# Mamba2 scan and low-rank mixer on one core: batch 0's up product by split halves

## The chip, the cores and the metric

The kernel runs on one core of a Trainium2 chip. The metric is the device time of one execution in microseconds. Before the change three runs took 219.5, 219.6 and 219.62 us; their median is 219.6 us.

The engines are named as in the profile: PE is TensorE (PEld its weight loads), DVE is VectorE, ACT is ScalarE, POOL is GpSimd, SP is SyncE, which here only issues DMAs.

## The reference

Two stages follow each other. The first is a chunked state-space scan over 4 batches, 8 heads, 768 positions, head size 32, state size 16. The second is a mixer over the tokens and a two-layer network over the channels:

```python
xt = x.transpose(0, 2, 1)
h = xt @ U @ V                      # over 768 positions, rank 32
u = x + h.transpose(0, 2, 1)        # (4, 768, 256)
ch = np.maximum(u @ w_ch1, 0.0) @ w_ch2   # 256 -> 1024 -> 256
return (u + ch).astype(np.float32)
```

The weights U, V, w_ch1 and w_ch2 reach the kernel as 64-bit floats, so each of their numbers is two 32-bit words in memory, and the kernel turns them into 32-bit numbers itself, by masks, integer operations and products on the two words.

## The kernel before

**An order written out by hand.** The kernel is under manual scheduling. A string PLAN of some 630 words is followed word by word (`follow`, L875); each word calls one function that emits a few instructions. Every engine runs its own instructions in that order, and waits only for the results it needs. So moving a word in PLAN moves its instructions on every engine's queue, and moving a load moves it on SP's queue.

**The scan.** The 768 positions of a batch are three pairs of blocks, so there are twelve pairs k = 0 to 11, three per batch. Words for pair k: `b` and `x` load B, C and x (SP); `P` (or `Q`, a part of it) scales B and C by decays into BC (`prep`, L471); `T` transposes BC on PE and ScalarE copies it out (L483); `g` is the gram product, `m` and `M` its causal masks on VectorE (L518, L531); `s` the chunk states and `u` their update, on VectorE, with a masked copy Sm made by GpSimd (L548, L563); `i`, `n`, `j` are products into the output y, with a tiny GpSimd copy `settled` (L590) that holds `j` behind `i`; `y` and `t` copy and transpose the result.

**The mixer.** Per batch b (`mixer`, L684): `p`, `q`, `a` apply U and V and add to u. Then come the up product (1024 columns as eight blocks m of 128, over two halves j of 384 tokens) and the down product `d` (L787). For batches 1 to 3 a 32-bit number is held as three parts, near, far and both, so that a product is made by three one-pass products in place of one plain 32-bit product, which runs in several passes. `S` (L730) splits u into these parts (one ScalarE, two VectorE instructions); `f` (L762) makes the first two products, two matmuls each, and ScalarE multiplies the sum in PSUM by 1 + EPS; `e` (L768) adds the third product and ScalarE takes the Relu; `h` and `J` split the result for the down product. Batch 0 before the change has a plain up product `U` (L751), two 32-bit matmuls for each (j, m), which appear as four instructions, and ScalarE takes the Relu; its down product is plain too (`PLAIN = 2`).

**Weights.** `W` and `w` load pieces of w_ch1 and w_ch2, 512 KB each but for two of 256 KB. `c` converts a piece to 32 bits, one step of the generator `to_fp32` (L412) for each word c: two masks on VectorE and a conversion on ScalarE; then the exponent on ScalarE; then two VectorE operations; then the product. Pieces c0 and c2 are the first quarter of w1 (columns 0 to 255, which are m = 0 and 1), c3 to c5 the other three quarters, c1 is U and V, c6 to c9 are the first four quarters used of w2. `R` (`refine`, L445) makes the parts near, far and both out of a converted quarter; R0 to R3 are w1's, R4 to R7 w2's, all for batches 1 to 3. Temporaries, loaded words and Relu results share fifteen buffers called `words`; the converted w1 (`w1f`) shares one buffer with u's parts.

The VectorE is reached through a wrapper, so that all VectorE instructions have line L162 in the profile. Line L740 is the matmul inside `products`, for U, f, e and d alike.

Of the kernel before, what the change touches and what calls it, by code (L numbers as in the profile page):

```python
# [10 lines left out]
FP32 = mybir.dt.float32  # L11
# [3 lines left out]
WCOLS = 512  # L15
# [19 lines left out]
    'b0.0 b0.1 b0.2 x0.0 x0.1 b1.0 b1.1 b1.2 ')  # L35
PLAN = (
# [43 lines left out]
def kernel(  # L80
# [185 lines left out]
    def load_w(n):  # L266
        if n < 2:
            if "w" not in own:
                own["w"] = words_of(w1f[0])
# [175 lines left out]
    def refine(c):  # L445
# [11 lines left out]
        if c >= NQ:  # L457
            yield
            far = low.bitcast(FP32)
            both.append(w2c(n, FP32R))  # L460
# [464 lines left out]
```

## Time and profile before

The page of the profile shows one execution, which took 220.41 us from outside; its span, from the first to the last instruction, is 218.7 us. In the tables of stretches the columns are the bounds in us, the length, the busy time (and number of instructions) of PE, PEld, DVE, ACT and POOL, the granted clock, the DMA share and GB/s. In rows of a timeline the columns are the start, the length, the engine, the line, what is written and read, the shape and the number of instructions merged; a merged row's length runs to the end of the last. In rows of groups the numbers behind the bar are the busy time in us and the mean of one in ns.

| what | us |
|---|---|
| median of the runs | 219.6 |
| the profiled execution, from outside | 220.41 |
| its span | 218.7 |
| TensorE busy in the span | 210.3 |
| VectorE busy | 154.0 |
| ScalarE busy | 114.2 |
| GpSimd busy | 17.7 |

Matmuls overlap, and their ends are modelled. So a matmul's cost is read from start to start, not from its length. On VectorE and ScalarE consecutive instructions overlap by a little under 0.1 us, so sums of their lengths are a little too long.

### The profile page before, as it was taken

How to read it: one execution, taken by the hardware profiler on the slowest of the kernel's cores; microseconds unless marked ns; L12 is line 12 of the kernel's file. 1: busy time of each engine (PE TensorE's matmuls, PEld its weight loads, DVE VectorE, ACT ScalarE, POOL GpSimd, SP SyncE). 2: the span in 40 equal slices, each digit the busy share in tenths (PEclk: the TensorE clock that was granted, in tenths of full speed). 3: DMA queues.
4: the chain of work that ended last, by engine and by line, in shares of the span. 5: the costliest groups of instructions: out<-in, count | busy, mean ns of one | idle time of the engine just before them, and what ended most of it. 6: DMA issues, size and time to landing. Idle time of an engine off the chain costs nothing.

```text
span 218.7 us, 6992 instructions
## 1 busy us (share of the span) xinstructions
PE 210.3 (96%) x2988; PEld 182.4 (83%) x2988; DVE 154.0 (70%) x330; ACT 114.2 (52%) x261; POOL 17.7 (8%) x41
## 2 busy tenths in 40 slices
PE   7999899999899999999999999999999999999993
PEld 4667566665677889998998999999999999999992
DVE  4687689999983996349796697566575945757813
ACT  3335967798357554645555458153565364466220
POOL 6021020010300210002120000100000000000000
PEclk9999999999999999999999999999999999999999
DMA  6986879896082170080000450100000010100003
GB/s 87 132 118 150 152 103 330 233 207 88 3 124 47 19 132 4 18 126 3 27 3 1 53 118 0 51 10 24 0 0 24 17 34 3 48 3 22 3 24 120
DMA packets 69519, 14.56 MB, mean 67 GB/s; under 512 B 63793, under 2 KB 67697, under 8 KB 69489
## 3 DMA queue, kind: packets, MB, share of 16 engines
q1 hardware_dynamic: 69488, 14.13, 32.5%
q8 instruction: 23, 0.38, 0.8%
q14 instruction: 8, 0.06, 0.1%
HBM read 10.98 MB, written 3.15 MB: 65 GB/s over the span
## 4 chain that ended last, share of the span: by engine, by line
PE 83%; DVE 11%; issue 2%; ACT 1%; DMA 1%; POOL 0%; DVEq 0%; POOLq 0%; ACTq 0%
PE x L740 27%; PE z L740 22%; PE y L740 12%; DVE words L162 5%; PE y L651 3%; PE y L629 3%; PE x L525 2%; PE w L671 2%; DVE M L162 2%; PE w L494 2%; DVE S L162 2%; PE w L557 1%; PE z L525 1%; PE w L694 1%; DMA a_sb<-in_a_dram 1%
## 5 line engine op out<-in xcount | busy, mean ns | idle before, releaser
L162 DVE SCALAR_TENSOR_TENSOR words<-words 128x768 fp32r<-128x768 f32 (+6 forms) x44 | 33.8, 799 | 0.3
L740 PE MATMUL x<-u,w 128*128 128x384 f32 x144 | 32.1, 342 | 0.0
L740 PE MATMUL z<-u,w 128*128 128x384 f32 x144 | 32.1, 342 | 0.0
L740 PEld LDWEIGHTS x<-u,w 128*128 128x128 f32 x144 | 24.6, 188 | 0.4 <-issue 0.2
L740 PEld LDWEIGHTS z<-u,w 128*128 128x128 f32 x144 | 24.3, 188 | 0.4 <-issue 0.2
L740 PE MATMUL x<-w2c,words 128*128 128x256 f32 x112 | 22.8, 339 | 0.7 <-DVE w2c L162 0.7
L745 ACT ACTIVATE x<-x 128x384 f32<-128x384 f32 (+1 forms) x30 | 13.6, 454 | 18.8 <-PE x L740 17.3
L745 ACT ACTIVATE z<-z 128x384 f32<-128x384 f32 (+1 forms) x27 | 12.5, 463 | 18.3 <-PE z L740 14.5
L740 PE MATMUL y<-w,words 128*128 128x256 f32 x144 | 20.3, 280 | 0.0
L740 PEld LDWEIGHTS x<-w2c,words 128*128 128x128 f32 x112 | 18.2, 189 | 2.4 <-DVE w2c L162 0.9
L162 DVE SCALAR_TENSOR_TENSOR words<-x,words 128x384 fp32r<-128x384 f32 x24 | 13.0, 552 | 9.7 <-ACT words L774 9.6
L740 PEld LDWEIGHTS y<-w,words 128*128 128x128 f32 x144 | 19.2, 188 | 0.0
L162 DVE SCALAR_TENSOR_TENSOR words<-z,words 128x384 fp32r<-128x384 f32 x24 | 12.8, 550 | 6.7 <-ACT words L774 6.7
L740 PE MATMUL x<-w,words 128*128 128x256 f32 x96 | 14.3, 285 | 0.0
L585 POOL TENSOR_TENSOR Sm<-S,own 128x256 f32<-128x256 f32 (+1 forms) x12 | 8.1, 676 | 76.3 <-DVE S L162 44.7
L774 ACT ACTIVATE words<-x 128x384 fp32r<-128x384 f32 x24 | 11.4, 488 | 5.6 <-PE x L740 5.6
L774 ACT ACTIVATE words<-z 128x384 fp32r<-128x384 f32 x24 | 11.3, 492 | 5.0 <-PE z L740 5.0
L162 DVE SCALAR_TENSOR_TENSOR S<-S,kept,w 128x64 f32<-128x64 f32 x40 | 11.2, 279 | 2.8 <-PE w L557 0.9
L740 PEld LDWEIGHTS x<-w,words 128*128 128x128 f32 x96 | 12.9, 189 | 0.1
L740 PE MATMUL z<-w2c,words 128*128 128x256 f32 x56 | 11.5, 339 | 0.2 <-DVE S L162 0.2
L651 PE MATMUL y<-M,x 64*32 64x64 f32 x768 | 10.5, 225 | 1.0 <-issue 0.9
L663 ACT COPY yT<-y 128x256 f32<-128x256 f32 x24 | 7.8, 380 | 6.9 <-PE y L629 6.9
(154 smaller groups left out, 400.0 us busy)
## 6 DMA issues: line engine op xcount, KB each, us to landing
words<-in_moe_w_ch_dram SPq DMA_DIRECT2D x7, 512.0 KB, 5.2
x<-in_x_dram SPq DMA_DIRECT2D x24, 128.0 KB, 3.4
out_dram<-ytok SPq DMA_DIRECT2D x24, 128.0 KB, 1.7
bc<-in_B_dram SPq DMA_DIRECT2D x24, 64.0 KB, 3.0
bc<-in_C_dram SPq DMA_DIRECT2D x12, 128.0 KB, 3.2
words<-in_moe_w_ch_dram SPq DMA_DIRECT2D x2, 256.0 KB, 3.7
words<-in_moe_V_dram SPq DMA_DIRECT2D x4, 48.0 KB, 1.9
words<-in_moe_U_dram SPq DMA_DIRECT2D x1, 192.0 KB, 4.0
```

What stands on the lines that cost most here:

```text
L162: self.last = call(*args, **kwargs)
L494: nc.tensor.transpose(out=tp[:, i, v], in_=s["BC"][:, i, c + v].rearrange("p h n -> p (h n)"), identity=ident)
L525: nc.tensor.matmul(out=g[r][cols, c], lhsT=s["T"][rows, 0, c, cols], rhs=s["Cm"][rows, :, :, ts(2 * c + p, Q)].rearrange("r v t i -> r v i ...
L557: nc.tensor.matmul(out=s["A"][p][ts(r, Q), v], lhsT=s["BC"][half, 0, v, 2 * r:2 * r + 2].rearrange("p h n -> p (h n)"), rhs=x_sb[k][half, ...
L585: nc.gpsimd.tensor_tensor(out=s["Sm"][:, sl], in0=s["S"][:, sl].rearrange("p i (s d) -> p i s d", s=2), in1=own2[:, b, 4 * q:4 * q + sl.st ...
L629: product = nc.tensor.matmul(out=y[p][ts(r % 2, H), r // 2, c], lhsT=own[ts(r, Q)], rhs=s["T"][ts(r, Q), 1, :, ts(2 * c + p, Q)].rearrange ...
L651: product = nc.tensor.matmul(out=y[p][ts(i, Q), n, c], lhsT=x_sb[k][half, c, h], rhs=s["M"][half, h // 2, c, h % 2], start=fresh(k, p, [i] ...
L663: nc.scalar.copy(out=yp[:, :, :, p], in_=st[k]["y"][p])
L671: nc.tensor.transpose(out=t[:, c, g], in_=yT[b][:, g, ts(2 * q + c, P)], identity=ident)
L740: nc.tensor.matmul(out=t, lhsT=lhsT, rhs=rhs, start=start, stop=True, skip_group_check=True)
L745: nc.scalar.activation(t, t, AF.Copy, scale=1.0 + EPS)
L774: nc.scalar.activation(gs[j, m // 2][0][:, m % 2], t, AF.Relu, scale=NEAR)
```

## The change

Three things change at once.

1. **Batch 0's up product.** For m = 2 to 7 the plain `U` becomes `f` and `e` as in the other batches, with `S0.0` and `S0.1` in front; the Relu's result isn't split, because batch 0's down product stays plain. For m = 0 and 1 `U` remains. So 4 `U`, 12 `f` and 12 `e` stand where 16 `U` stood. The pieces c3 to c5 are no longer converted to one 32-bit number: a new generator `to_parts` makes near, far and both from the two words directly, in six steps. `R1`, `R2` and `R3` go. The first quarter is converted as before into `w1f`, now one of the fifteen `words` buffers.
2. **Additions on GpSimd.** In `to_parts` an integer addition and the difference for both; in `to_fp32` of the w2 pieces (`aside`) an integer addition in place of VectorE's addition; in `refine` both differences (now four steps); and `prep` of pairs 4 to 11.
3. **Order.** The whole PLAN from the second line on. Among it the loads: W3, W2 and W4 stand ahead of most of b4, b5 and x4, and c4 is begun before c3.

```diff
+SCALED = range(4, 12)
 PLAN = (
...
-    w1all = mix.tile([P, NQ, NCB, W], FP32, tag="u", name="w1f", bufs=1)
-    w1f = [w1all[:, c] for c in range(NQ)]
+    w1f = raw.tile([P, 2 * WCOLS], INT32, tag="words", name="w1f", bufs=NWORDS).bitcast(
+        FP32)[:, :NCB * W].rearrange("p (c m) -> p c m", c=NCB)
...
+        if aside:
+            nc.gpsimd.tensor_tensor(out=rest, in0=top, in1=rest, op=ALU.add)
         nc.scalar.activation(power, e, AF.Relu, bias=bias[:p], scale=8.0)
         yield
-        vector.scalar_tensor_tensor(out=rest, in0=top.bitcast(FP32), scalar=-7.0 * 2 ** 20,
-                                       in1=rest, op0=ALU.add, op1=ALU.add)
+        if not aside:
+            vector.scalar_tensor_tensor(out=rest, in0=top.bitcast(FP32), scalar=-7.0 * 2 ** 20,
+                                           in1=rest, op0=ALU.add, op1=ALU.add)
...
+    def to_parts(dst, words):
...
+        vector.tensor_scalar(out=head, in0=hi, scalar1=0x7ffffe00, scalar2=None,
+                                op0=ALU.bitwise_and)
+        vector.tensor_scalar(out=low, in0=hi, scalar1=0x1ff, scalar2=3,
+                                op0=ALU.bitwise_and, op1=ALU.logical_shift_left)
+        nc.scalar.activation(rest, lo.bitcast(UINT32), AF.Copy, scale=2.0 ** -29)
+        yield
+        nc.gpsimd.tensor_tensor(out=rest, in0=low, in1=rest, op=ALU.add)
+        nc.scalar.activation(power, head, AF.Relu, bias=bias[:p], scale=8.0)
+        yield
+        vector.scalar_tensor_tensor(out=power, in0=hi, scalar=-2 ** 31, in1=power,
+                                       op0=ALU.bitwise_and, op1=ALU.bitwise_or)
+        yield
+        nc.scalar.copy(out=near, in_=wide(power.bitcast(FP32)))
+        vector.tensor_scalar(out=head, in0=power, scalar1=-2 ** 23, scalar2=None,
+                                op0=ALU.bitwise_and)
+        yield
+        vector.scalar_tensor_tensor(out=far, in0=wide(rest), scalar=2.0 ** -11,
+                                       in1=wide(head.bitcast(FP32)), op0=ALU.mult, op1=ALU.mult)
+        yield
+        nc.gpsimd.tensor_tensor(out=both, in0=wide(power.bitcast(FP32)), in1=far.bitcast(FP32),
+                                op=ALU.subtract)
+        yield
...
-        vector.tensor_tensor(out=far, in0=w, in1=near.bitcast(FP32), op=ALU.subtract)
+        nc.gpsimd.tensor_tensor(out=far, in0=w, in1=near.bitcast(FP32), op=ALU.subtract)
+        yield
         nc.scalar.activation(low, far, AF.Copy, scale=1.0 / EPS)
...
+        nc.gpsimd.tensor_tensor(out=both[0], in0=near.bitcast(FP32), in1=low.bitcast(FP32),
+                                op=ALU.subtract)
...
-            vector.tensor_tensor(
+            (nc.gpsimd if k in SCALED else vector).tensor_tensor(
                 out=part, in0=bc_sb[k].rearrange("p h i c n -> p (i c) h n")[:, g],
...
         def second(j, m):
 
+            t = gs["t", j, m]
+            products(t, terms(j, m, (2,)), False)
+            if not (b or j >= PLAIN):
+                if (j, m // 2) not in gT:
+                    gT[j, m // 2] = pair(FP32)
+                nc.scalar.activation(gT[j, m // 2][:, m % 2], t, AF.Relu)
+                return
```

The stretch of PLAN on which the prediction dwells, from the first up product on, reads before (to its last up product):

```
U0.0.0 m4 c4 U0.0.1 P5 c4 c5 U0.1.0 U0.1.1 c5 w7 B6 U0.1.3 T5 M4 U0.1.2 s4 u4.0 c4 n4 u4.1 s5 c6 R1 R0
c5 L7 u5.0 T5 c9 u5.1 c7 U0.0.2 c5 c9 c7 U0.1.5 c7 c6 c6 c6 U0.0.3 U0.0.4 U0.1.4 U0.1.6 c8 P6 c8 U0.0.6
c8 U0.1.7 c7 d0.1.2.0 c8 c9 i4 g5 m5 T6 c9 d0.1.2.1 d0.1.2.2 T6 L8 M5 d0.1.2.3 U0.0.5 n5 R0 i5 P7 j4 g6
y4.0 X6 y4.1 R1 R3 j5 t4 d0.1.1.0 M6 P8 y5.1 T7 m6 y5.0 R2 R5 U0.0.7
```

and after:

```
U0.0.0 c4 c4 c3 T4 T4 c4 U0.1.0 P5 c3 U0.0.1 U0.1.1 f0.0.4 w5 X5 c5 c5 c3 g4 t3 e0.0.4 B6 m4 c3 f0.0.5
c5 M4 c3 f0.0.2 c5 s4 n4 T5 T5 e0.0.2 c5 u4.0 u4.1 c5 f0.0.6 e0.0.5 f0.0.7 i4 c6 R0 g5 j4 y4.0 M5 c6
y4.1 P6 e0.0.6 m5 c6 f0.0.3 s5 u5.0 w6 n5 c6 T6 u5.1 e0.0.7 T6 d0.0.0.0 e0.0.3 i5 R4 g6 w7 m6 w8 S0.1 j5
c7 y5.0 y5.1 t4 M6 d0.0.1.0 c7 L7 f0.1.2 P7 f0.1.3 t5 L8 f0.1.7 c7 f0.1.6 f0.1.4 d0.1.0.0 c8 e0.1.3 c8 c9
c7 e0.1.2 e0.1.6 d0.0.0.1 f0.1.5 d0.0.1.1 c8 c8 e0.1.7 e0.1.5 p1 c9 X6 T7 c9 d0.0.2.0 c9 e0.1.4
```

More of the change, by code (lines that the diff above doesn't have):

```diff
@@ L268, in load_w @@
             if "w" not in own:
-                own["w"] = words_of(w1f[0])
-            dst, t = w1f[0][:, :, ts(n, P)], own["w"][:, ts(n, 2 * NCB * P)]
+                own["w"] = words_of(w1[0][:, :, ts(0, W)])
+            dst, t = w1f[:, :, ts(n, P)], own["w"][:, ts(n, 2 * NCB * P)]
             weights[2 * n] = dst, t
@@ L274, in load_w @@
         elif n <= NQ:
-            load_words(n + 1, w1f[n - 1], w13[:, :, ts(n - 1, 2 * quarter)])
+            dst = each(w1, every, every, ts(n - 1, W))
+            t = words_of(dst[0])
+            weights[n + 1] = dst, t
+            begin(out=t.rearrange("p (i j) -> p i j", i=NCB),
+                  in_=w13[:, :, ts(n - 1, 2 * quarter)])
         else:
@@ L449, in refine @@
             w2, every, ts(n, 2))
-        w = (w1f if c < NQ else w2f)[n]
+        w = w1f if c < NQ else w2f[n]
+        if c >= NQ:
+            both.append(w2c(n, FP32R))
         nc.scalar.activation(near, w, AF.Copy, scale=NEAR)
@@ L749, in pair, with terms @@
             return t.bitcast(dtype)[:, :2 * HS].rearrange("p (m t) -> p m t", m=2)
+        def terms(j, m, which):
+            return [(w1[v][:, n, ts(m, P)], us[j][v][:, n]) for v in which for n in range(NCB)]
         def plain(j, m):
@@ L755, in plain @@
             t = bank("xz"[m % 2], HS)
-            products(t, [(w1f[m // 2][:, n, ts(m % 2, P)], block(n, j)) for n in range(NCB)], True)
+            products(t, [(w1f[:, n, ts(m, P)], block(n, j)) for n in range(NCB)], True)
             nc.scalar.activation(gT[j, m // 2][:, m % 2], t, AF.Relu)
-        def terms(j, m, which):
-            return [(w1[v][:, n, ts(m, P)], us[j][v][:, n]) for v in which for n in range(NCB)]
         def first(j, m):
```

44 lines of the change are left out of this document (28 added, 16 removed), and 75 rows, old and new, of the table PLAN.

## The prediction

> **What bounds the kernel now.** I read the profile page's engine shares and its chain of waits first, then the busy time by stretches, then the waits of TensorE.
>
> ```profile
> span 218.7 us, 6992 instructions
> PE 210.3 (96%) x2988; PEld 182.4 (83%) x2988; DVE 154.0 (70%) x330; ACT 114.2 (52%) x261; POOL 17.7 (8%) x41
> PE 83%; DVE 11%; issue 2%; ACT 1%; DMA 1%; POOL 0%; DVEq 0%; POOLq 0%; ACTq 0%
> ...
> 30.00:40.00 10.00, 9.79 (x111) 6.30 (x93) 9.09 (x22) 7.28 (x17) 0.52 (x1) 1.00 0.99 257
> 34.90:67.70 32.80, 32.09 (x414) 21.26 (x413) 30.35 (x66) 23.06 (x48) 3.85 (x4) 1.00 0.70 149
> ...
> PE x L740 <- DVE w2c L162: 0.7, 1, 0.7
> ```
>
> TensorE holds 83% of the chain. Batch 0's sixteen plain up products (U) lie between 34.9 and 67.7 us, and in that stretch TensorE misses only 0.7 of 32.8 us, at full clock; its one long wait there is for a down weight of VectorE (0.7 us). So TensorE's own work sets the end, and work taken off it counts in full as long as nobody starves it. But VectorE is 93% busy there (30.35 of 32.8), and DMA 99% from 30 to 40 us: the feeding engines are close behind.
>
> **TensorE's gain.** The two ways of multiplying stand side by side in the trace, as start-to-start times.
>
> ```profile
> 48.48 5.32 PE L740 MATMUL x<-yT,w1f 128*128 128x384 f32 x16
> 53.64 1.45 PE L740 MATMUL z<-yT,w1f 128*128 128x384 f32 x4
> ...
> 88.09 0.86 PE L740 MATMUL z<-u,w 128*128 128x384 f32 x4
> 88.79 0.51 PE L740 MATMUL x<-u,w 128*128 128x384 f32 x2
> 89.13 0.86 PE L740 MATMUL z<-u,w 128*128 128x384 f32 x4
> ```
>
> A plain product is 4 instructions; 16 of them take 53.64 - 48.48 = 5.16 us, so one product 1.29 us. The split one, as batch 1 makes it, is 4 instructions (0.70) and then 2 (0.34): 1.04 us. Twelve of sixteen change: 12 x (1.29 - 1.04) = 3.0 us; by the finer 0.174 us of one instruction, 12 x 0.245 = 2.94 us, which I take. The four left plain stay at 1.29.
>
> **What that asks of ScalarE.** New: 12 rescalings in PSUM between f and e, two S (near part of u), three copies of w1's near part. Gone: the two passes of R1, R2 and R3.
>
> ```profile
> L745 ACT ACTIVATE x<-x 128x384 f32<-128x384 f32 x24 | 11.4, 476 | 17.5 <-PE x L740 16.3 <-ACT yT L663 0.8 <-DVE words L162 0.2
> L757 ACT ACTIVATE words<-x 128x384 f32<-128x384 f32 x8 | 3.7, 489 | 0.0
> L735 ACT ACTIVATE u<-yT 128x768 fp32r<-128x768 f32 x6 | 5.0, 839 | 3.3 <-DVE yT L162 3.3
> L451 ACT ACTIVATE w<-w1f 128x512 fp32r<-128x512 f32 x4 | 2.4, 637 | 0.0
> ```
>
> 12 x 0.476 + 2 x 0.839 + 3 x 0.637 - 3 x 2 x 0.637 (the second pass of R has the same size as the first) = +5.5 us over the kernel. If all of it fell on the old stretch, ScalarE would hold 23.06 + 5.5 = 28.6 us against TensorE's 32.8 - 2.94 = 29.9; the end still belongs to TensorE, with only 1.3 us to spare. Each new half product has f, a rescaling, e and a Relu in a row, 0.476 + 0.489 = 0.97 us of ScalarE beside 1.04 of TensorE, so ScalarE now paces almost as tightly as TensorE; that is a rival below.
>
> **VectorE's relief.** The removed and added instructions:
>
> ```profile
> L162 DVE TENSOR_TENSOR BC<-bc,F 128x512 f32<-128x512 f32 x9 | 6.2, 684 | 0.5 <-issue 0.5
> L162 DVE TENSOR_TENSOR words<-w1f,w 128x512 f32<-128x512 f32 x4 | 2.7, 682 | 0.0
> L162 DVE SCALAR_TENSOR_TENSOR w<-words,w 128x512 fp32r<-128x512 f32 x4 | 3.1, 766 | 0.1
> L162 DVE SCALAR_TENSOR_TENSOR w2c<-w,w 128x512 fp32r<-128x512 f32 x4 | 2.7, 680 | 0.0
> L162 DVE SCALAR_TENSOR_TENSOR words<-words 128x512 f32<-128x512 f32 x7 | 4.8, 685 | 0.1
> L162 DVE TENSOR_SCALAR words<-words 128x512 int32<-128x512 int32 x14 | 6.1, 476 | 0.0
> L162 DVE SCALAR_TENSOR_TENSOR u<-u 128x768 fp32r<-128x768 f32 x6 | 5.8, 958 | 0.2
> L162 DVE TENSOR_TENSOR u<-yT,u 128x768 fp32r<-128x768 f32 x6 | 5.7, 955 | 1.3 <-ACT u L735 1.2
> ```
>
> Off VectorE: P4 to P11 (8 x 0.684 = 5.5); the refinement of w1 (4 x 1.448 = 5.8) and of w2 (4 x (0.682 + 0.680) = 5.4; its first pass has the size of w1's); one addition in each of four w2 conversions (4 x 0.685 = 2.7); in each of the three w1 quarters an addition becomes a masking (3 x 0.21 = 0.6). On it: S0.0 and S0.1, 2 x 1.913 = 3.8. Net -16.2 us of 154. That is no gain by itself where TensorE is dense; it pays at most the 0.7 us wait shown above, and I take nothing of it.
>
> **GpSimd's load, and the turns it takes with VectorE.** GpSimd gets 8 P, 6 passes of w1's quarters, 4 additions for w2 and 2 passes in each of five refinements: 28 operations of 128x512. No row shows that size.
>
> ```profile
> 13.48 0.62 POOL L585 TENSOR_TENSOR Sm<-S,own 128x256 f32<-128x256 f32 x1 [2.86 <-DVE S L162]
> 20.79 0.51 POOL L585 TENSOR_TENSOR Sm<-S,own 128x192 f32<-128x192 f32 x1 [1.06 <-DVE S L162]
> 24.15 0.19 POOL L592 COPY settled<-slot 128x1 f32<-128x1 f32 x1 [2.85 <-PE y L651]
> 56.55 2.13 POOL L592 COPY settled<-slot 128x1 f32<-128x1 f32 x1 [6.82 <-PE y L629]
> 71.79 0.93 POOL L585 TENSOR_TENSOR Sm<-S,own 128x256 f32<-128x256 f32 x1 [7.56 <-DVE S L162]
> ...
> 57.35 1.28 DVE L162 SCALAR_TENSOR_TENSOR words<-words 128x512 f32<-128x512 f32 x2
> 72.28 0.99 DVE L162 SCALAR_TENSOR_TENSOR w<-words,w 128x512 fp32r<-128x512 f32 x1
> ```
>
> From the undisturbed pair, 64 columns cost 0.11 us, so 512 cost 0.62 + 4 x 0.11 = 1.06 us. The upper end is twice the slowed one at 71.79, 1.86 us. I take 1.06, being nearest to an operation that waits for nobody: 28 x 1.06 = 30 us over some 90 us (from the first w1 quarter to P11). By the Trainium skill (GPSIMD Engine Reference, section Elementwise — side-by-side cycle accounting) a two-input addition of 2048 columns takes 4497 ns; a quarter of that, 1.12 us, would be an estimate close to mine.
>
> The last rows show that the two engines block each other. A copy that takes 0.19 us took 2.13 beside back-to-back two-input operations of VectorE, and ended when these ended (57.35 + 1.28 = 58.63); at 71.79 GpSimd was held 0.31 us, and then VectorE's next one took 0.99, where its group has 0.77 on the mean with this one in it. The Trainium skill (SBUF — State Buffer, section Who interferes with whom) says why: a VectorE instruction with two SBUF inputs and a GpSimd instruction that reads SBUF exclude each other for their whole length. The trace agrees. By that rule work moved from VectorE to GpSimd isn't taken out of the way but made longer, 0.68 to 1.06 us in the same queue for a port.
>
> So I add the port's load over the new plan's stretch from U0.0.0 to e0.1.4, the last half product of batch 0, and TensorE's in the same words.
>
> ```profile
> 64.76 0.66 PE L671 MATMUL w<-ident,yT 128*128 128x128 f32 x4
> 65.25 1.03 PE L740 MATMUL z<-w2c,words 128*128 128x256 f32 x4
> 66.11 0.38 PE L494 MATMUL w<-ident,BC 128*128 128x128 f32 x2
> 66.33 1.46 PE L740 MATMUL z<-yT,w1f 128*128 128x384 f32 x4
> ...
> 69.09 0.79 PE w L694 x16
> ```
>
> VectorE's SBUF work: four w2 conversions (2 x 0.476 + 2 x 0.685 = 2.32 each, 9.3), what is left of three w1 quarters (5.8 by the same two prices) and S0.1 (1.9): 17.0. GpSimd: 9 passes of conversions, P5 to P7 and two Sm, 12 x 1.06 + 0.62 + 0.51 = 13.9. Together 30.9 us. TensorE: 4 x 1.29 + 12 x 1.04 = 17.6; the scan, turning and down work that the old stretch holds beside its U, 32.8 - 16 x 1.29 = 12.2; and what the new stretch has more, two T (0.22 each, from 66.11 to 66.33), two t (twice 0.49, from 64.76), a d (0.86) and p (0.79), 4.0, beside a gram: 33.8 at the least. The port has less to do than TensorE, so it delays little in sum; masks and state updates read PSUM and can go beside GpSimd. I take 0.
>
> What queues behind: a refinement's or conversion's addition waits for ScalarE, and GpSimd then holds up the P behind it (T and gram wait for that) and the Sm (i and j on TensorE). Those have the down pieces d0 and plain U as cover; without it each such delay is one operation, about 1.06 us.
>
> **Loads.** Three 512 KB pieces of w1 move ahead of b4, b5 and x4 on SP's queue.
>
> ```profile
> 32.72 0.47 SPq L188 DMA_DIRECT2D x<-in_x_dram  x1
> 42.98 0.45 PE L557 MATMUL w<-x,BC 64*32 64x64 f32 x32
> ACT words L430 <- DMA words<-in_moe_w_ch_dram: 0.7, 1, 0.7
> ```
>
> At the 257 GB/s of 30 to 40 us a piece is 2.0 us, so x4 lands up to 6 us later; it was issued at 32.72 for a use at 42.98, so this hides. The conversions now begin before the old 0.7 us wait. I put the front at nothing, between -1 us (conversion and p0, q0 start earlier) and +1 (u4's inputs late).
>
> **Sum.** -2.94 + 0. The profiled execution took 220.41 us with a span of 218.7; the median is 219.6, 0.8 lower. The change is taken from the median: 216.7 (the profiled one would be 217.5).
>
> **The rivals.** *ScalarE paces the new half products.* For: 0.97 against 1.04 us, with conversions, T and y between. Against: TensorE has d0 and scan work to slip in. Price: in half of the six units of the first 384 tokens, where the conversions are thickest, e waits for a whole rescaling with nothing beside it, 3 x 0.476 = 1.4 us: 218.1. *TensorE's gain is not on the path*, since conversions set the pace (VectorE 93%): the 2.94 us become idle, 219.6. Against: VectorE sheds 16 us. *The port, slower than before.* Between U0.0.0 and the last batch 0 half product VectorE and GpSimd take turns, VectorE's strict order keeping its PSUM work (12 masks at 0.417 and 7 updates at 0.28, 7.0 us) from filling the gaps:
>
> ```profile
> L162 DVE TENSOR_TENSOR M<-x,causal 128x256 int32<-128x256 int32 x24 | 9.0, 417 | 0.6 <-PE z L525 0.5
> L162 DVE SCALAR_TENSOR_TENSOR S<-S,kept,w 128x64 f32<-128x64 f32 x40 | 11.2, 279 | 2.8 <-PE w L557 0.9
> ```
>
> With 1.06 a piece that is 30.9 + 7.0 = 37.9, or 4.1 us beyond TensorE's 33.8; with 1.46, midway to 1.86, 42.7, or 8.9 beyond. Less the 2.94 saved, that is +1.2 to +6.0; I take the middle, less 1.0 for the gram left out of 33.8: +2.6, so 222.2. It decides from where the shared work passes 33.8 + 2.94 = 36.7 us, which full turns reach at 1.06 already. For: the blocking rows. Against: it shows only where VectorE runs back to back, and VectorE has less to do now.
>
> **How the numbers follow.** Forecast (215.4 to 217.8) 0.50; ScalarE 0.18; no gain 0.08; port 0.24. A difference under 0.2% (0.44 us) can't be told from none. Faster takes the forecast, ScalarE's case and a little of the third: 0.68; same 0.06; slower 0.26. The range runs from 214.6 (the front's -1 and the 0.7 of the wait won, and 0.4 in hand for what GpSimd takes off VectorE later) to 222.4, which takes in the port's price.
>
> **What would show it.** Right: 12 batch 0 half products in place of 12 plain ones, TensorE idle by under 1 us after its first U, GpSimd's 128x512 operations mostly near 1.1 us, the last product of batch 0's up stage and p1 close together in time. ScalarE's rival: TensorE waits on "x" or "z" of the rescaling. The port: GpSimd operations of 2 us and more, VectorE ones lengthened, TensorE waiting for w or BC. The prediction is wrong if TensorE's waits between U0.0.0 and the last batch 0 product add up to over 3 us, or if the first U starts more than 1 us later than 34.9.

## The result, and the profile after

The changed kernel takes 226.41 us (four runs, 225.75 to 227.37) against 219.61 for the kernel before: by the means of the runs 1.0295 times as long, with a 95% interval of 1.0229 to 1.0361. The forecast was 216.7, its range 214.6 to 222.4; the time is above both. The profiled execution took 225.88 us with a span of 224.0, 5.3 us longer than the span before.

The page of the changed kernel: busy time by engine, tenths of the span in forty slices for two of its rows, and the chain of waits. The two rows behind them are the same ones of the kernel before.

```profile
span 224.0 us, 7065 instructions
PE 210.4 (94%) x3012; PEld 185.0 (83%) x3012; DVE 148.8 (66%) x307; ACT 119.5 (53%) x272; POOL 50.8 (23%) x69
PE   7979778879989999999999999999999999999994
POOL 6021035558128614052490101000000000000000
PE 68%; DVE 13%; SPq 10%; DMA 3%; issue 2%; ACT 2%; POOL 1%; DVEq 0%; POOLq 0%
```

```profile
PE   7999899999899999999999999999999999999993
POOL 6021020010300210002120000100000000000000
```

TensorE's share of the chain fell from 83% to 68%, and its row has sevens and eights from the fifth to the ninth slice (22 to 50 us); GpSimd's row, nearly empty before, has threes to eights from the sixth to the tenth. The stretches show how much each lost. The bounds are the first U, the first matmul of p1, p2 and p3, and the end; first the kernel before, then the changed one:

```profile
0.00:34.90 34.90, 31.12 (x750) 21.47 (x751) 25.16 (x81) 18.26 (x50) 7.62 (x25) 1.00 0.80 138
34.90:69.00 34.10, 33.40 (x421) 22.20 (x419) 30.35 (x66) 24.36 (x51) 3.85 (x4) 1.00 0.67 143
69.00:117.80 48.80, 48.61 (x744) 44.25 (x743) 35.17 (x73) 25.12 (x56) 5.25 (x8) 1.00 0.22 37
```

```profile
0.00:34.40 34.40, 28.31 (x710) 18.83 (x710) 25.36 (x81) 17.61 (x48) 9.00 (x27) 1.00 0.93 148
34.40:71.20 36.80, 32.89 (x474) 25.70 (x474) 29.50 (x54) 28.80 (x61) 18.32 (x17) 1.00 0.58 108
71.20:124.10 52.90, 52.61 (x738) 47.09 (x737) 31.18 (x61) 27.58 (x61) 20.73 (x21) 1.00 0.32 53
```

The words between two bounds aren't the same in the two orders, so a length alone doesn't tell what was lost. I compared the words of PLAN in each stretch and priced the difference by TensorE's start-to-start times. Over the whole PLAN TensorE's work falls by the 2.94 us of the twelve products. Ahead of the first U the changed kernel leaves out T4 twice, g4 and t3 (0.22 us each, 0.98 from 33.45 to 34.43 us of the kernel before, and 0.49: about 1.9) and gets there 0.5 us sooner: 1.4 us lost at the front. From the first U to p1 twelve U at 1.29 are gone, twelve f at 0.70 and eleven e at 0.34 are new, a T, the gram and the t come in (1.7) and one down piece less stands there (about 1.0): 2.7 us less to do, and it takes 2.7 us longer, 5.4 lost. From p1 to p3 another 1.4 are lost, behind p3 nothing. 1.4 + 5.4 + 1.4 - 2.94 = 5.3, the difference of the spans. Most of what p1 to p2 takes longer (48.8 to 52.9) is work that moved there.

The 1.4 us at the front come from one profile of each order, and the start of the first U varies by more: with the same instructions ahead of it, it came at 34.4, 34.5 and 37.1 us in three profiles with the new order (the changed kernel and two runs below), at 34.9, 33.4 and 35.4 with the old one. So that part isn't clear of the spread.

TensorE's waits and the timeline of the changed kernel show how the loss looks:

```profile
PE x L796 <- DVE w L164: 2.1, 2, 1.4
```

VectorE's only wait for a result of GpSimd from 34 to 76 us, and rows of the timeline:

```profile
DVE w2c L164 <- POOL words L447: 1.2, 1, 1.2
```

```profile
37.53 1.85 POOL L483 TENSOR_TENSOR words<-words 128x512 int32<-128x512 int32 x1 [2.31 <-DVE words L164]
38.29 1.91 DVE L164 SCALAR_TENSOR_TENSOR u<-u 128x768 fp32r<-128x768 f32 x1
41.41 1.66 POOL L496 TENSOR_TENSOR w<-words,w 128x512 fp32r<-128x512 f32 x1 [2.03 <-DVE w L164]
41.85 3.09 DVE L164 TENSOR_SCALAR words<-words 128x512 int32<-128x512 int32 x3
45.53 1.09 DVE L164 SCALAR_TENSOR_TENSOR w<-words 128x512 fp32r<-128x512 int32 x1
46.67 0.62 PE L796 MATMUL x<-u,w 128*128 128x384 f32 x2 [1.38 <-DVE w L164]
```

An integer addition of GpSimd (L483) and the second half of S0.0 on VectorE (u<-u) overlap: the one takes 1.85 us, the other 1.91, where its group had a mean of 0.96 before. Then three masks of VectorE take 3.09 us beside the difference for both (L496) and P5, which runs on GpSimd from 43.02 to 44.32 us; three by the mean before are 1.4. The far part that they push back (at 45.53) is the `w` for which TensorE waits 1.38 us at 46.67. The timeline names no wait of VectorE between 36 and 50 us; the one for GpSimd came after 69. So TensorE waits there for a VectorE whose own operations have grown longer, not for a GpSimd result on its way. The run without the additions below gives the means without them (958, 444 and 686 ns); against these, VectorE's rows from 38.29 to 48.65 us are an estimated 3.5 us too long.

### The profile page after: what moved, and what is told of

Same layout as the page of the kernel before. It is cut to its first block, busy times and chain, and to the rows that moved or that the text cites. A ratio compares the mean times of both kernels' runs of the same rounds, so it can differ in the third digit from the quotient of the medians.

```text
span 224.0 us, 7065 instructions
## 1 busy us (share of the span) xinstructions
PE 210.4 (94%) x3012; PEld 185.0 (83%) x3012; DVE 148.8 (66%) x307; ACT 119.5 (53%) x272; POOL 50.8 (23%) x69
## 4 chain that ended last, share of the span: by engine, by line
PE 68%; DVE 13%; SPq 10%; DMA 3%; issue 2%; ACT 2%; POOL 1%; DVEq 0%; POOLq 0%
PE x L796 26%; PE z L796 18%; PE y L796 12%; SPq L190 10%; DVE words L164 6%; DMA words<-in_moe_w_ch_dram 3%; PE y L685 2%; DVE u L164 2%; PE y L707 2%; PE w L550 1%; PE w L727 1%; PE w L750 1%; DVE w L164 1%; PE x L581 1%; PE w L613 1%
## 5 line engine op out<-in xcount | busy, mean ns | idle before, releaser
L796 PE MATMUL x<-u,w 128*128 128x384 f32 x180 | 41.5, 349 | 2.3 <-DVE w L164 2.1
L796 PE MATMUL z<-u,w 128*128 128x384 f32 x180 | 41.9, 348 | 0.2 <-DVE words L164 0.2
L164 DVE SCALAR_TENSOR_TENSOR words<-words 128x768 fp32r<-128x768 f32 (+5 forms) x37 | 33.2, 915 | 4.5 <-ACT words L448 2.9
L796 PEld LDWEIGHTS x<-u,w 128*128 128x128 f32 x180 | 30.8, 188 | 4.4 <-DVE w L164 2.8
L796 PEld LDWEIGHTS z<-u,w 128*128 128x128 f32 x180 | 30.7, 188 | 1.4 <-DVE words L164 0.5
L801 ACT ACTIVATE x<-x 128x384 f32<-128x384 f32 (+1 forms) x36 | 16.5, 460 | 18.3 <-PE x L796 17.8
L801 ACT ACTIVATE z<-z 128x384 f32<-128x384 f32 (+1 forms) x33 | 15.4, 466 | 16.4 <-PE z L796 12.7
L641 POOL TENSOR_TENSOR Sm<-S,own 128x256 f32<-128x256 f32 (+1 forms) x12 | 7.2, 600 | 34.7 <-DVE S L164 34.7
L648 POOL COPY settled<-slot 128x1 f32<-128x1 f32 x12 | 3.7, 304 | 45.7 <-PE y L685 43.0
L164 DVE TENSOR_SCALAR words<-words 128x512 int32<-128x512 int32 (+2 forms) x23 | 11.6, 549 | 1.2 <-DMA words<-in_moe_U_dram 1.1
```

The costliest lines, as they stand in the source:

```text
L164: self.last = call(*args, **kwargs)
L641: nc.gpsimd.tensor_tensor(out=s["Sm"][:, sl], in0=s["S"][:, sl].rearrange("p i (s d) -> p i s d", s=2), in1=own2[:, b, 4 * q:4 * q + sl.st ...
L648: op = nc.gpsimd.tensor_copy(out=settled, in_=slot[:, :1])
L796: nc.tensor.matmul(out=t, lhsT=lhsT, rhs=rhs, start=start, stop=True, skip_group_check=True)
L801: nc.scalar.activation(t, t, AF.Copy, scale=1.0 + EPS)
```

## The experiments

Each stretch named below is read from the rows of that run as above: from the first U to the first matmul of p1 (34.1 us before, 36.8 changed), and from p1 to p2 (48.8 and 52.9).

### What was moved, put back on VectorE

Theory: GpSimd's operations are the loss, so undoing them wins the time back. Four runs of the changed kernel, all in its new order: P of pairs 4 to 11 back, the ten operations of the conversions back, the ten differences of the refinements back, and all 28.

```diff
-SCALED = range(4, 12)
+SCALED = range(0)
...
-            nc.gpsimd.tensor_tensor(out=rest, in0=top, in1=rest, op=ALU.add)
+            vector.tensor_tensor(out=rest, in0=top, in1=rest, op=ALU.add)
...
-        nc.gpsimd.tensor_tensor(out=rest, in0=low, in1=rest, op=ALU.add)
+        vector.tensor_tensor(out=rest, in0=low, in1=rest, op=ALU.add)
...
-        nc.gpsimd.tensor_tensor(out=far, in0=w, in1=near.bitcast(FP32), op=ALU.subtract)
+        vector.tensor_tensor(out=far, in0=w, in1=near.bitcast(FP32), op=ALU.subtract)
```

> The changed kernel with prep of pairs 4 to 11 back on VectorE (SCALED empty); nothing else. Port theory (VectorE's SBUF work and GpSimd's exclude each other, and the lengthened VectorE starves TensorE between the first U and p1): 8 operations of 1.10 us leave the port and 8 of 0.68 return to VectorE, three of them in that stretch and P4 just ahead of a0; the wait ahead of the first U falls by the 0.8 us by which P4 lengthened VectorE's mask, and about 1.5 us in all are won: 224 to 225.5 us. Rival (the half products and the new order starve TensorE by ScalarE and by dependencies, whatever the engine): no change or slower by VectorE's 2 us in the stretch: 226 to 228.

> The changed kernel with the ten additions and differences of the conversions c3 to c9 back on VectorE. Port theory: these are the ones that meet VectorE's own conversion steps in the stretch, 1.3 to 1.9 us each on GpSimd against 0.68 on VectorE, so most of the 4.9 us lost there comes back: 222 to 224 us. Rival (dependencies and ScalarE): 226 to 228, since VectorE gets 6.8 us more to do.

> The changed kernel with both differences of the refinements R0 and R4 to R7 back on VectorE. Most of them run after p1, where TensorE lost only 1.4 us. Port theory: little, 225.5 to 226.5 us, VectorE being free enough there. Rival: the same; this run only sizes the part.

> The changed kernel with all 28 operations back on VectorE, order and half products kept. Port theory: the lengthening of VectorE (7.1 us between the first U and p1) is gone and 13 x 0.68 = 9 us of its own work come back there, so a part of the loss remains: 221 to 224 us. Rival (half products and order themselves): 226 us or more, as VectorE is loaded by 20 us more in all. If it falls under 219.6 the half products pay by themselves.

Measured against the kernel before (220.48 in these runs): P back 233.63 us, 1.0618 (1.0534 to 1.0701); conversions back 228.7, 1.0356 (1.0268 to 1.0444); refinements back 229.26, 1.0403 (1.0342 to 1.0465); all back 239.31, 1.0835 (1.0751 to 1.0919). None wins time back, and the theory in this form falls. P and all 28 back cost clearly more than the changed kernel; the intervals of the other two overlap its own (1.0229 to 1.0361). The stretches say the same: from the first U to p1 43.1 us with P back, 40.6 with the conversions back, 43.9 with all, against 36.8; with the refinements back it stays at 36.8, and p1 to p2 takes 55.7 in place of 52.9. The waits of VectorE and TensorE between 34 and 76 us with all 28 back, and then the group of VectorE's masks of the conversions in the whole span:

```profile
DVE BC L164 <- DMA bc<-in_B_dram: 4.4, 1, 4.4
PE x L796 <- DVE w2c L164: 4.7, 1, 4.7
```

```profile
L164 DVE TENSOR_SCALAR words<-words 128x512 int32<-128x512 int32 x17 | 7.0, 446 | 0.0
```

P in VectorE's queue waits 4.4 us there for a piece of B that the new order loads late, and the w2 conversion behind it in that queue then holds TensorE for 4.7. On GpSimd the same wait stands beside VectorE's work. So the order and the places of the operations belong together, in these runs. The last row, where GpSimd does nothing large, gives the masks 446 ns; in the changed kernel the same 17 take 632.

### What was moved, left out

If the operations can't be put elsewhere, leaving them out on every engine shows what they cost in this order. First the seven additions and the three differences of the conversions; the parts of w1 and w2 have other values then, and the near part stands in for both of w1. Second, twelve rescalings of batch 0's half products (ScalarE's rival). Third, the first set and the ten differences of the refinements as well; the near part then stands in for both of w2 too.

```diff
         if aside:
-            nc.gpsimd.tensor_tensor(out=rest, in0=top, in1=rest, op=ALU.add)
+            pass
...
-        nc.gpsimd.tensor_tensor(out=rest, in0=low, in1=rest, op=ALU.add)
...
-        nc.gpsimd.tensor_tensor(out=both, in0=wide(power.bitcast(FP32)), in1=far.bitcast(FP32),
-                                op=ALU.subtract)
```

> The changed kernel without the ten GpSimd operations of the conversions c3 to c9, on no engine: the low word's share is then missing from w1 (three quarters) and w2, and the third product reads near or far in place of both. This takes 13.6 us from GpSimd, nothing from the other engines. Contention theory (VectorE lengthened by 7.1 us between the first U and p1, beside GpSimd's 1.3 to 1.9 us operations, and TensorE waiting 4.4 us there): the stretch falls from 36.8 to about 33.5 us, the time to 222.5 to 224. Theory that the chain of conversion, half products and ScalarE alone starves TensorE: under 1 us, 225.5 or more.

```diff
-            scaled(t)
+            if b or j >= PLAIN:
+                scaled(t)
```

> The changed kernel without the twelve rescalings by 1 + EPS in batch 0's half products (the factor is left out of these sums). 5.7 us less of ScalarE, and e follows f without a round through ScalarE. ScalarE theory: TensorE's waits for ScalarE between the first U and p1 go, 1.5 to 3 us, 223.5 to 225. Contention theory: VectorE's conversions remain late, under 0.7 us, about 226.

```diff
-        nc.gpsimd.tensor_tensor(out=far, in0=w, in1=near.bitcast(FP32), op=ALU.subtract)
...
-        nc.scalar.activation(low, far, AF.Copy, scale=1.0 / EPS)
+        nc.scalar.activation(low, w, AF.Copy, scale=1.0 / EPS)
...
-        nc.gpsimd.tensor_tensor(out=both[0], in0=near.bitcast(FP32), in1=low.bitcast(FP32),
-                                op=ALU.subtract)
```

> The changed kernel without any of its moved additions and differences: the seven additions and three differences of the conversions and the ten differences of the refinements are left out on every engine, so the values of w1 and w2 are other ones; P of pairs 4 to 11 stays on GpSimd, and the order stays. A ceiling for the change: if the split halves do bring TensorE's 2.9 us and the additions, wherever they stand, are what eats it, the stretches lose their idle time (33 to 34 us from the first U to p1, 50 to 52 from p1 to p2), and the time is 219 to 222, above the forecast by what the front lost. If it stays at 225 or more, something else than the additions holds the new order.

Without the conversions' ten operations the four runs spread from 221.26 to 226.88 us (220.08 to 222.97 for the kernel before), so their total says little; the stretch from the first U to p1 took 33.6 us: 3.2 less than with them, as expected. Without the rescalings that stretch took 36.6 against 36.8 us, and the whole kernel 227.74 us, 1.0307 (1.0228 to 1.0386): ScalarE doesn't pace it. Without all twenty additions and differences the time was 223.79 us, 1.0154 (1.0105 to 1.0202). Three views of that run: its busy line, the same two stretches, and the groups of the conversions' masks and of S's second half on VectorE. The stretch row of the run without the rescalings stands behind its two for comparison:

```profile
PE 211.8 (95%) x3012; PEld 187.7 (84%) x3012; DVE 141.4 (64%) x307; ACT 119.1 (54%) x272; POOL 22.8 (10%) x49
```

```profile
36.50:69.60 33.10, 32.32 (x475) 26.23 (x474) 25.29 (x53) 28.71 (x62) 4.95 (x7) 0.98 0.63 117
69.60:122.60 53.00, 52.30 (x742) 47.22 (x743) 28.57 (x60) 27.51 (x61) 6.98 (x11) 1.00 0.33 55
```

```profile
37.10:73.70 36.60, 33.46 (x476) 25.96 (x475) 29.27 (x54) 24.03 (x50) 18.17 (x17) 0.98 0.55 106
```

```profile
L164 DVE SCALAR_TENSOR_TENSOR u<-u 128x768 fp32r<-128x768 f32 x8 | 7.7, 958 | 0.3
L164 DVE TENSOR_SCALAR words<-words 128x512 int32<-128x512 int32 x17 | 6.8, 444 | 0.0
```

In the changed kernel the same groups read:

```profile
L164 DVE TENSOR_SCALAR words<-words 128x512 int32<-128x512 int32 x17 | 10.0, 632 | 0.0
L164 DVE SCALAR_TENSOR_TENSOR u<-u 128x768 fp32r<-128x768 f32 x8 | 8.6, 1077 | 0.3
```

VectorE runs the same 307 instructions in both and is busy 148.8 us beside the additions, 141.4 without them: 7.4 us of VectorE's time are lengthening by these operations. From the first U to p1 the stretch falls from 36.8 to 33.1 us, 3.7 less, and VectorE's busy time in it from 29.50 to 25.29: so these operations eat TensorE's gain there. The first U came 2.1 us later in this profile than in the changed kernel's, but a late start doesn't shorten the stretch: without the rescalings the first U came at 37.1 us and the stretch still took 36.6. From p1 to p2 nothing changes (53.0 against 52.9). What is left beyond that, the front and 1.4 us behind p1, doesn't come from the additions. Even without them the kernel is slower than before, so they are only a part of the loss: 3.7 of the 5.4 us in the stretch, and nothing that shows elsewhere.

### The moves alone, in the order before

The kernel before, with its plain products and its PLAN, and only the operations on GpSimd: first P of pairs 4 to 11, both differences of the eight refinements and the additions of seven conversions, 31 in all; then each set by itself; then the refinements of w2 only.

```diff
-            vector.tensor_tensor(
+            (nc.gpsimd if k in SCALED else vector).tensor_tensor(
...
-        vector.tensor_tensor(out=far, in0=w, in1=near.bitcast(FP32), op=ALU.subtract)
+        nc.gpsimd.tensor_tensor(out=far, in0=w, in1=near.bitcast(FP32), op=ALU.subtract)
...
-                steps[c] = to_fp32(*weights[c], c - 2 - NQ)
+                steps[c] = to_fp32(*weights[c], c > 2)
```

> The kernel before, its order and its plain up products, with the second part of the change alone: prep of pairs 4 to 11, both differences of all eight refinements and one addition in each of the seven conversions c3 to c9 on GpSimd. Contention theory: VectorE and GpSimd meet in the same stretch as in the changed kernel, VectorE is lengthened by 5 us or more between the first U and p1 and the time rises to 222 to 226, without any half product. Theory of the half products and the order: VectorE is relieved by some 18 us, and nothing is lost: 218.5 to 220.

> The kernel before, with P of pairs 4 to 11 on GpSimd and nothing else changed (the run with all 31 operations moved took 236.0 us, 47.3 us from the first U to p1 in place of 34.1). Theory 'each operation that takes turns costs its share': 8 of 31 moved operations, so about a quarter of the 15 us, 223 to 225 us. Rival 'only an operation that stands between two steps of a conversion costs, because VectorE's next step waits for it': P has no VectorE step behind it, only T on TensorE, so 219.5 to 221 us. VectorE's lengthened operations from the first U to p1: under 2 us by the second.

> The kernel before, with both differences of each of its eight refinements (16 operations) on GpSimd and nothing else changed. By shares: 16 of 31, some 8 us, 227 to 229. By the rival (a chain VectorE to GpSimd to ScalarE to GpSimd costs only where a later VectorE step waits): only far and both for the half products of batches 1 on wait, none of them in batch 0, so 219.5 to 222 us, with the loss, if any, behind p1.

> The kernel before, with only the additions of the seven conversions c3 to c9 (7 operations of 1.28 us) on GpSimd. By shares: 7 of 31, 3 to 4 us, 223 to 224. By the rival (VectorE's last step of a piece waits for GpSimd, and everything of VectorE behind it waits too) this is the part that costs most, 226 to 232 us, with VectorE waiting for GpSimd's words and TensorE for w1f between the first U and p1.

```diff
+        aside = nc.gpsimd if c >= NQ else vector
...
-        nc.gpsimd.tensor_tensor(out=far, in0=w, in1=near.bitcast(FP32), op=ALU.subtract)
+        aside.tensor_tensor(out=far, in0=w, in1=near.bitcast(FP32), op=ALU.subtract)
```

> The kernel before with the differences of the four w2 refinements on GpSimd (8 operations), those of w1 back on VectorE. In the run with all 16 moved, TensorE waited 4.1 us for two tiny GpSimd copies (settled) that stood behind a w1 difference waiting for ScalarE. If this queue is the cause, the w2 half costs nearly nothing: 219.5 to 222 us, 34 to 35 us from the first U to p1. If turns with VectorE are the cause, half of the 7.9 us stays: 223 to 225.

| on GpSimd | us | ratio (95%) | first U to p1 |
|---|---|---|---|
| nothing (before) | 219.06 to 223.47 in these runs | 1 | 34.1 |
| P of 4 to 11 | 221.98 | 1.0046 (1.0005 to 1.0087) | 36.4 |
| seven additions of conversions | 223.53 | 1.0129 (1.0054 to 1.0204) | 35.6 |
| all refinements | 228.8 | 1.037 (1.0317 to 1.0423) | 40.4 |
| refinements of w2 only | 222.19 | 1.0065 (1.0031 to 1.01) | 35.4 |
| all of them | 236.0 | 1.0667 (1.0601 to 1.0733) | 47.3 |

The stretches come from one profiled execution each, and with the refinements moved that one took 225.76 us, 3 below the median. How far a stretch varies by itself can be read from the run with w2's refinements: none of its eight differences falls between the first U and p1 (GpSimd does four instructions there, 3.91 us, as before with 3.85), and yet the stretch took 35.4 us:

```profile
35.40:70.80 35.40, 33.76 (x421) 22.08 (x419) 30.33 (x66) 24.42 (x51) 3.91 (x4) 1.00 0.68 147
```

By number of operations (8, 7 and 16 of 31) the three sets would cost 3.9, 3.4 and 7.8 us of the 15.1. The conversions (2.6) and the refinements (7.9) took about that, as the expectations by shares had it; P (1.0) took less, and within the refinements w2's eight took 1.3, which leaves most to w1's eight, though these weren't run alone. P's time lies between its two expectations. So the number alone doesn't decide. VectorE's lengthening doesn't decide alone either: with the conversions' additions moved VectorE was busy 31.66 us in the stretch, against 30.35 before, although it did 59 instructions there against 66, and the stretch grew by 1.5 us only. GpSimd's timeline with all refinements moved, and what TensorE waited for, say what w1's cost:

```profile
62.48 1.26 POOL L460 TENSOR_TENSOR w<-w,w 128x512 fp32r<-128x512 f32 x1 [4.26 <-ACT w L456]
63.68 0.19 POOL L591 COPY settled<-slot 128x1 f32<-128x1 f32 x1
...
65.83 1.74 POOL L460 TENSOR_TENSOR w<-w,w 128x512 fp32r<-128x512 f32 x1 [0.74 <-ACT w L456]
67.51 0.18 POOL L591 COPY settled<-slot 128x1 f32<-128x1 f32 x1
```

```profile
PE y L628 <- POOL settled L591: 4.1, 2, 2.8
```

A difference (L460) waits 4.26 us for ScalarE at the head of GpSimd's queue. Behind it stands the copy `settled`, 0.19 us long, that lets TensorE begin `j`: TensorE stops for 4.1 us in two waits. VectorE was busy 28.21 us in that stretch, 2.1 less than before, where the four operations gone are 2.9: turns cost it little. So for w1's refinements in the old order it is GpSimd's queue, more than turns: 4.1 us of waits in a stretch that grew by 6.3. The run with w2's refinements alone has no such wait, but it can't decide between queue and turns as the expectation meant it to, since its differences run behind p1. In the changed kernel, where R1 to R3 are gone and the order is another, TensorE waits 0.5 us for `settled` in all.

With everything moved (236.0 us, more than either expectation had) the wait rows name 4.7 us for `settled` and 3.1 for `w2c`, and the granted clock fell as well; the row of the stretch, whose PE time rose from 33.40 to 38.59 us at a mean clock of 0.89:

```profile
35.80:83.10 47.30, 38.59 (x425) 24.85 (x425) 27.04 (x51) 25.16 (x51) 22.81 (x19) 0.89 0.51 105
```

### The front and the loads

What loses time ahead of the first U? (The expectation below reckons 1.9 us lost from 2.4 us of work left out; by the rows above it is 1.4 from 1.9.) The chain of waits of the changed kernel from 24 us on (start, length, what) names a load and VectorE's order:

```profile
24.64 6.43 DMA words<-in_moe_w_ch_dram
...
31.09 0.69 ACT words L481
...
32.24 1.55 DVE words L164 x2
...
33.82 1.95 DVE yT L164 x4
```

The first steps of c4 wait for W3, and the two masks of that step, lengthened to 1.55 us beside P4, stand ahead of the additions to yT (a0) for which the first U waits. Two edits of the new PLAN try this, the one in the order of the engines, the other in the order of the loads:

```diff
-c2 q0 n3 i3 c4 x4.0 a0.0 j3 a0.1 y3.0 b5.0 x4.1 P4 c4 c2 c4 c3 S0.0 y3.1 U0.0.0 c4 c4 c3 T4 T4 c4 U0.1.0
+c2 P4 q0 n3 i3 x4.0 a0.0 j3 a0.1 c4 y3.0 b5.0 x4.1 c4 c2 c4 T4 T4 c3 S0.0 y3.1 g4 t3 U0.0.0 c4 c4 c3 c4 U0.1.0
```

> The changed kernel with the old order ahead of the first U: P4 before q0, the first step of c4 behind a0.1, and T4, the gram g4 and t3 ahead of U0.0.0, where the kernel before has them. By the work that TensorE has done at the first U, the new order starts 1.9 us late (2.4 us less work done, 0.5 us earlier). If the order is what lost it: 1 to 2 us won, 224.4 to 225.5. If the start is set by loads and conversions whatever the order: no change, 226 or more.

```diff
-c1 W3 b4.1 t1
+c1 b4.1 x4.1 W3 t1
```

> The changed kernel with two loads put ahead of W3 again, b4.1 and half of x4, nothing else. If the order of the loads costs the front its 1.9 us, u4 and P4 wait less and the time falls by 1 to 2 us, to 224.5 to 225.5. If instead the piece W3 is what is scarce there (c4 is the first piece that is converted), the piece comes about 2 us later, the first f waits for it, and the time rises to 227 to 229.

The first took 230.07 us, 1.0407 (1.0344 to 1.047). GpSimd's P4 now waits for C, TensorE for `settled` behind P4 and then for the turned C, and the granted clock is 0.50 (a row of GpSimd, two of TensorE, and the stretch from 34 to 42 us):

```profile
32.63 1.10 POOL L534 TENSOR_TENSOR BC<-bc,F 128x512 f32<-128x512 f32 x1 [1.01 <-DMA bc<-in_C_dram]
```

```profile
33.91 0.69 PE L685 MATMUL y<-T,Sm 32*64 32x64 f32 x12 [0.31 <-POOL settled L648]
38.64 0.47 PE L581 MATMUL x<-Cm,T 32*64 32x128 f32 x2 [2.24 <-ACT Cm L560]
```

```profile
34.00:42.00 8.00, 5.34 (x56) 4.03 (x57) 6.63 (x11) 4.47 (x9) 2.58 (x2) 0.50 0.55 102
```

The second took 227.84 us, 1.0299 (1.0229 to 1.0368). The time lies where the second theory had it (the piece W3 is what is scarce), but the ratio is that of the changed kernel (1.0295): nothing is won, and a loss isn't shown either. In its chain of waits W3 lands at 33.75 us in place of 31.07, the masks and yT follow, and the first U waits 1.77 us for yT, where the changed kernel's waited 0.59:

```profile
27.86 5.89 DMA words<-in_moe_w_ch_dram
...
33.78 0.76 DVE words L164 x2
...
34.57 1.49 DVE yT L164 x3
```

Neither edit won the front back: one of W3 and pair 4's B, C and x is late in any of the three orders. Whether another order avoids it wasn't tried.

### The halves alone

Is the loss the moves', would the halves alone have won? An order of my own: the PLAN before, its `U` for m = 2 to 7 replaced by f and e (half 1 first, since u's parts have one buffer), S0.1 and S0.0 in front of them, R1 to R3 gone, all additions on VectorE; then the same with P and the w1 pieces' additions and differences on GpSimd.

```diff
-U0.1.3 T5 M4 U0.1.2 s4
+f0.1.3 T5 M4 f0.1.2 e0.1.3 s4
...
-U0.0.3 U0.0.4 U0.1.4 U0.1.6 c8 P6 c8 U0.0.6 c8 U0.1.7
+f0.1.7 e0.1.4 f0.1.6 e0.1.7 e0.1.6 S0.0 c8 P6 c8 f0.0.3 c8 f0.0.2 e0.0.3
```

> The first part of the change alone: split halves for m = 2 to 7 of batch 0, every addition on VectorE as before, the order of before but for the new words (half 1 first, then half 0, S0.1 and S0.0 in front; R1 to R3 gone). Reckoned from rows of before, VectorE gets 3 x 1.2 us for the three pieces and 2 x 1.9 us for the two S, and loses 3 x 1.45 us: +3.1 us on the 30.4 us of 32.8 that it had, while TensorE loses 2.9. Theory 'VectorE is what the change runs into, so the moves to GpSimd were forced': VectorE sets the stretch, which takes 33.5 to 36 us, and the time is 219.5 to 222. Rival 'the halves alone would have won, the moves spoiled it': TensorE's gain arrives, 216.5 to 218.

> The same, with P of pairs 4 to 11 and the addition and the difference of the three w1 pieces (14 operations) on GpSimd, the refinements and the w2 additions left on VectorE. If a share of the moves helps where VectorE is the bound, 217 to 219.5 us, better than the halves alone. If every GpSimd operation beside VectorE costs VectorE about its own length, the same as the halves alone or up to 3 us more, 220 to 224.

They took 258.95 us, 1.1713 (1.163 to 1.1795), and 259.34, 1.1759 (1.17 to 1.1818). Neither expectation holds. Part of that isn't the change's: in these two kernels `e` of batches 1 to 3 makes the third product twice. TensorE has 3108 matmuls in place of the changed kernel's 3012, and behind p1 the first run takes 169.7 us where the changed kernel takes 152.8, 16.9 more, or 0.176 for each of the 96. Less these 17 us the first would be an estimated 242 us, still far behind. The rest arises ahead of p1, where batch 1 has no e yet. The page's busy line, the waits and the stretch of the first show that this order is bad by itself: TensorE waits for the rescaling of the product before, or for u's parts (1.9 us), and works at a mean clock of 0.81.

```profile
PE 234.6 (91%) x3108; PEld 207.2 (80%) x3108; DVE 158.7 (61%) x334; ACT 122.0 (47%) x272; POOL 16.5 (6%) x41
```

```profile
PE z L784 <- ACT z L789: 5.6, 3, 2.9
```

```profile
35.70:88.70 53.00, 40.85 (x449) 30.34 (x450) 36.66 (x74) 30.14 (x63) 2.86 (x4) 0.81 0.45 93
```

So these two runs don't tell what the halves alone would bring in an order tuned for them; that stays open. They show only that f and e put where U stood starve TensorE: the stretch to p1 takes 53.0 us. None of the sixteen runs was faster than the kernel before.

## Why the prediction was wrong

**TensorE's gain, -2.94 us: right.** Twelve products changed, and neighbouring instructions of batch 0's half products follow each other as priced; eight of them in the changed kernel:

```profile
64.67 1.57 PE L796 MATMUL x<-u,w 128*128 128x384 f32 x8
```

That is seven steps of 0.177 us and the last one's own 0.33. It reached the stretch, in part, only where the additions were left out: 33.1 us, where the kernel before has 34.1 for 2.7 us more of work. The total stayed above the kernel before even there.

**ScalarE's load: right in size, and its rival falls.** ScalarE was busy 28.80 us from the first U to p1, where the prediction had 28.6 for the old stretch; without the rescalings that stretch was 0.2 us shorter, not 1.4.

**GpSimd's price: a little low.** Estimated at 1.06 us a piece, with 1.86 as the upper end; P's shortest are 1.10 us, the integer additions' 1.28, the refinements' about 1.27, both's of w1 1.45. In the stretch it is the dearer ones that stand there. In the mean, with the waits for VectorE in them, P took 1.13 and both's of w1 1.59.

**The step that failed: "The port has less to do than TensorE, so it delays little in sum … I take 0."** The sums were not far off and the conclusion is wrong. At the shortest lengths measured GpSimd's share of the port is 6 x 1.28 + 3 x 1.45 + 3 x 1.10 + 1.13 = 16.5 us in place of 13.9, so the port has 33.5. On TensorE's side what the new stretch has more adds up to 3.1 us as listed, not 4.0; the 4.0 and the 33.8 come out only with the gram counted in. So the port was near TensorE's load, still not above it. But sums compare engines that could work whenever they like. Here a piece of w1 passes from VectorE to ScalarE to GpSimd and back, f waits for its far part and e for both, and every mask that a GpSimd operation lengthens pushes back what stands behind it in VectorE's strict order; TensorE's longest named wait in the stretch, 1.38 us, is f's for the far part. The stretch lost 5.4 us against the one before, of which 3.7 go when the additions and differences do (3.2 without the conversions' alone). The prediction's own rows (a 0.19 us copy stretched to 2.13, a VectorE operation to 0.99) were the warning. By the Trainium skill (SBUF — State Buffer, section Who interferes with whom) a VectorE instruction with two SBUF inputs and a GpSimd instruction that reads SBUF exclude each other. The trace agrees: the addition L483 ends at 39.38 us, 1.13 us after the first half of S0.0 on VectorE (37.30 to 38.25), and the second half ends 0.82 us after L483. To call 16.2 us VectorE's relief was therefore wrong too: VectorE's busy time fell by 5.2 us (154.0 to 148.8), and by 12.6 without the additions (141.4).

**The second step: "I put the front at nothing."** The first U came at 34.4 us, as forecast, but with 1.9 us less of TensorE's work done: 1.4 lost in this pair of profiles, which the spread of the first U (over 2 us with the same instructions ahead of it) doesn't let me call shown. The sign that I named, a first U later than 35.9, could not see this, since the new order put work behind it. "It hides" was said of x4; it was B, C and W3 that came late for P4 and c4, and c4 stood ahead of a0.

**The rival that went the right way** was the port, with 222.2 us and a chance of 0.24. Two of its signs came: VectorE operations lengthened, and TensorE waiting for w (2.1 us). The third, GpSimd operations of 2 us and more, didn't; the longest took 1.85. The sign against the forecast came as well: TensorE's named waits behind the first U and up to p1 add up to 3.8 us, over the 3 that I set. The rival's price was too low: +2.6 in all, or +3.6 without the 1.0 taken off for a gram that 33.8 already held. Before the 2.94 are taken off that is 5.5 or 6.5, where the spans give 8.2 (5.4 in its stretch, 1.4 at the front and 1.4 behind, of which it had only the first). Within its stretch that is about what was lost, but only 3.7 of it go with the additions. The 1.4 us between p1 and p3 stay without a shown cause; they are there without the additions too. The 1.7 us of the 5.4 that the additions don't explain are open as well; P on GpSimd, which stayed in that run, wasn't taken out of it.

## What to carry to other kernels

Work moved from VectorE to GpSimd is not out of VectorE's way: price the VectorE operations that will run beside it by rows in which the two engines already overlap, and lay them along the chain in which the pieces are due, not against a sum. Look in the receiving queue for the small instruction that releases another engine, and ask what can wait at the head in front of it. And a stretch that begins on time may still have begun with less done; count the work ahead of it too, and take more than one profile before you call a start early or late.

## What the runs showed of the hardware

A mask of VectorE with one input, 128x512, took 444 to 446 ns without GpSimd's additions and 632 on the mean beside them, although it has only one operand in SBUF to read; the lengthening was not confined to instructions with two.

Where TensorE waited often, a lower granted clock was seen as well. In the run with P4 ahead of q0, TensorE was busy 2.94 and 2.91 of 4 us from 26 to 30 and 30 to 34 us, and the granted clock was 0.50 from 34 to 42 us, with named waits of 2.24 us or less. With all moves in the old order it was 0.89 over 47.3 us, and TensorE's busy time in the stretch rose by 5.2 us (33.40 to 38.59) for nearly the same 420 matmuls. What sets the clock isn't shown: the changed kernel was busy 3.07 of 4.4 us just ahead of its first U and kept 1.00.
